# Threshold attention with a LayerNorm feed-forward block: two PSUM banks ordered by hand, and the order of work around a Strassen chain

## The chip, the cores and the metric

The kernel runs on one core of a Trainium2 chip. The metric is the device time of one execution in microseconds. A core has five engines with a queue of instructions each: TensorE (PE in the profile; its weight loads are PEld), VectorE (DVE), ScalarE (ACT), GpSimd (POOL) and SyncE (SP), which issues most DMAs. Engines wait for each other by semaphores.

## The reference

Attention over 8 batches, 8 heads, 576 tokens and 64 features per head, in which only the scores within `tau` of the row's largest are kept. Then, per token over all 512 features, a normalisation, a hidden layer of 2048 with a ReLU, and a sum with the input:

```python
scores = scale * np.matmul(q, k.transpose(0, 1, 3, 2))
thresh = np.max(scores, axis=-1, keepdims=True) - tau
scores = np.where(scores >= thresh, scores, -1000000000.0)
attn = np.exp(scores - np.max(scores, axis=-1, keepdims=True))
attn = attn / (np.sum(attn, axis=-1, keepdims=True) + 1e-09)
x = heads_side_by_side(np.matmul(attn, v))          # (8, 576, 512)
xn = (x - mean(x)) / np.sqrt(var(x) + 1e-06) * g_ln
out = x + np.maximum(xn @ w_ch1, 0.0) @ w_ch2
```

All arithmetic on the chip is in float32. The weights come as float64 bits and are turned into float32 in the kernel.

## The kernel before

**Attention in slots.** The attention of one batch is nine slots, 72 in all (n = 0 to 71). A slot handles 256 query rows of two heads, or, in the fifth slot of a batch, the last 64 rows of every head. In a slot, TensorE makes the scores (L414) into two score tiles `sc`, VectorE reduces their negated maxima (`neg`, L433), GpSimd makes the thresholds (`thr`, L437), ScalarE makes four exponentials (L445) into a room `e`, VectorE masks and sums them (L454), GpSimd divides them (L470), and VectorE transposes them in blocks of 32 (L539, two instructions). Then a DMA writes them to DRAM (`scr`, L547), and others read them back in another order (`em` at L561, `er` at L566). The values matmuls of the slot (L605, L615) run one slot later. Slots 0 to 5 do the transposition on TensorE (`tp`, `tr`) instead.

There are two rooms for `e`. Slots 0 to 6 use them in turns; from slot 7 on all use room 0, and room 1 is taken over: first as two pieces in which raw weights are fetched (`conversion.take`), later, from group 1's first part on, for one of the sums of weights. The exponentials of a slot can only be written to a room when the `scr` DMA of the slot that used it has landed.

**Feed-forward groups.** Half a batch, 288 tokens, is a group, 16 in all (g = 0 to 15). Even groups are ready after the batch's fifth slot, odd ones after its ninth. The mean comes from a matmul with a constant matrix (`mean_of`), and VectorE subtracts it (`centre`, L680). `first_part` makes the hidden layer in tiles of 128 hidden features (`p1`, 16 matmul instructions each, then a ReLU on ScalarE, L917). Groups from 2 on do eight such tiles (t = 0 to 7), and the other half of the hidden layer in a `chain`: a Strassen product, two rounds of seven segments of 16 matmul instructions, in which a pair of banks is copied out by ScalarE after each segment (L857 to L883) while later segments go on adding into the same bank. Four of the segments in each round need a difference or a sum of inputs (`turns`, L821), and three per round need an add and a maximum afterwards (`rectify`, L842 and L843, on GpSimd). The variance is a square on ScalarE (L923), three adds on GpSimd (L925), a matmul (`var`) and three activations (L937 to L939). The second product of groups from 1 on is a Strassen product too (`second_quarters`, seven segments `seg` of 64 matmul instructions each, copied out at L1012).

**The order.** It is written out by hand, and engines follow it. Each slot has four quarters; in each, `second_part` issues as many steps of the feed-forward generator as its share (`ROOM`) allows, in between the slot's own work:

```python
rest = exponentials(n)                      # neg, thr
for _ in range(0 if chained[0] else 2):     # two exponentials at once
    next(rest)
second_part(n, 0)
while not chained[0] and next(held, None):  # the other two
    pass
second_part(n, 1)
diags = weights(es, thr, blocks_go)         # masks
second_part(n, 2)
scr = turn_blocks(b, s, room)               # L539 and the scr DMA
run(n, 3)                                   # values of the slot before
second_part(n, 3)
```

While `chained[0]` is set, an exponential is issued only after each finished tile or segment. VectorE's and GpSimd's closing work of a group's second product (adds, `finish` at L1047 and L1039, transposes of the output at L723) is kept in a list, `drops`, and issued in portions; `drip(everything=True)`, which `chain` calls first, issues all that is left. Of the odd groups from 3 to 13, tile 0 is begun in quarter 0 of a batch's third slot, and seven drops (two `finish`, one add, four output transposes) wait at that time.

**The banks.** Of the banks of PSUM, six hold the two score tiles with the values' outputs behind them. Two are left for everything else; they are a pool with two buffers under one tag (`ff`), and the framework chooses which of the two a new tile gets.

Of the kernel before, what the change touches and what calls it, by code (L numbers as in the profile page):

```python
# [18 lines left out]
def kernel(  # L19
# [39 lines left out]
    J = 4  # L59
# [15 lines left out]
    ps_sc = ctx.enter_context(tc.tile_pool(name="ps_sc", bufs=1, space=bass.MemoryType.PSUM))  # L75
    ps_ff = ctx.enter_context(tc.tile_pool(name="ps_ff", bufs=2, space=bass.MemoryType.PSUM))

# [110 lines left out]
    class Weights:  # L188
# [13 lines left out]
        def __init__(self):  # L202
# [29 lines left out]
            for t, n, before in (  # L232
# [7 lines left out]
                for p in range(n):  # L240
# [3 lines left out]
                    )  # L244

        def take(self, t):
            for p in range(2):
                self.free.append((2 * self.n1, -1, t[:, p * 2 * WC : (p + 1) * 2 * WC], 99))

# [174 lines left out]
    def exponentials(n):  # L424


        neg = small.tile([128, 4], F32, tag="neg", name="neg")
        thr = small.tile([128, 4], F32, tag="thr", name="thr")
        room = e_room[(n + 1) % 2 if n <= FIRST else 0]
        es = by_columns(room) if by_blocks(n) else by_rows(room)  # L430
        for h in range(2):
            i = slice(2 * h, 2 * h + 2)
            nc.vector.tensor_reduce(  # L433
                out=neg[:, i], in_=pairs[h],
                axis=AXL.X, op=ALU.max, negate=True,
            )
            nc.gpsimd.tensor_scalar(  # L437
                out=thr[:, i], in0=neg[:, i], scalar1=-1.0, scalar2=low_sb,
                op0=ALU.mult, op1=ALU.add,
            )  # L440
            if h == 0 and not chained[0]:
                run(n, "copy")
        for i in range(4):
            yield room, es, thr
            nc.scalar.activation(  # L445
                es[:, i], as_in(es, blocks[i]), func=AF.Exp, bias=neg[:, i : i + 1]
            )
# [36 lines left out]
    def turn_weights(s, es, diags):  # L484
# [3 lines left out]
        for i in range(4):  # L488
            if i:
                yield  # L490
            tp = ps_ff.tile([128, J, 128], F32, tag="ff", name="tp")
            for c in range(J):
                product(
                    tp[:, c], lhsT=es[:, i, c * 128 : (c + 1) * 128], rhs=diags[i],
                    start=True, stop=True,
                )
            if s == HP:
                nc.scalar.copy(
                    em[:, :, :, 32 * i : 32 * i + 32].rearrange("p a c x -> p c a x"),
                    tp.rearrange("p c (a x) -> p c a x", a=4),  # L500
                )
            else:
                h, j = divmod(i, 2)
                nc.scalar.copy(
                    em[:, 2 * j : 2 * j + 2, :, 64 * h : 64 * h + 64].rearrange("p a c x -> p c a x"),
                    tp.rearrange("p c (a x) -> p c a x", a=2),
                )
        tr = ps_ff.tile([128, 2, 128], F32, tag="ff", name="tr")
        for i in range(4):
# [69 lines left out]
    def values_of(b, s, turned_weights):  # L579
# [4 lines left out]
        if at_once:  # L584
            both = ps_ff.tile([128, 2, 128], F32, tag="ff", name="pv")
            pv = [both[:, j] for j in range(2)]
# [79 lines left out]
    def mean_of(g):  # L666
        if banks_taken[0]:
            waiting_mean.append(g)
            return
        means[g] = ps_ff.tile([128, TOK], F32, tag="ff", name="mean")  # L670
        product(means[g], lhsT=avg_sb, rhs=sums.pop(g), start=True, stop=True)

    def centre(g):
# [5 lines left out]
        for c in range(NK):  # L679
            nc.vector.tensor_tensor(  # L680
                out=xc[:, c], in0=groups[g][:, c], in1=mean, op=ALU.subtract
            )


# [118 lines left out]
    def chain(g, xc):  # L803
# [24 lines left out]

        def segment(bank, weights, rhs, ds, first):
            for i, d in enumerate(ds):  # L830
                for c in range(2):
                    at, end = (i, c), (len(ds) - 1, 1)
                    product(
                        bank[:, i], lhsT=weights(c, d), rhs=rhs[:, c],
                        start=first and at == (0, 0), stop=at == end,
# [4 lines left out]

        def rectify(eng, t, other):
            eng.tensor_tensor(out=t, in0=t, in1=other, op=ALU.add)  # L842
            eng.tensor_scalar(  # L843
                out=t, in0=t, scalar1=0.0, scalar2=1.0, op0=ALU.max, op1=ALU.mult
            )

        for n, at in enumerate(range(0, len(CHAIN), 2)):
            ds = CHAIN[at : at + 2]
            banks = [ps_ff.tile([128, 2, HT], F32, tag="ff", name="ch") for _ in range(2)]
            one, two = banks if n % 2 == 0 else banks[::-1]  # L850
            up, down = (hidden[:, ds[0] + o : ds[0] + o + 2] for o in (0, ND // 2))
            m1, u2, m7 = (None,) * 3
            part_tile = lambda name: ffn.tile([128, HM, HT], F32, tag="part", bufs=4, name=name)
            chained[0] = True
            yield from segment(one, a11, b11, ds, True)
            m1 = part_tile("m1")
            nc.scalar.copy(m1, one)  # L857
            yield 2, 0.5
            yield from segment(two, a12, b21, ds, True)
            nc.scalar.copy(up[:, :, early], two)  # L860
            rectify(nc.gpsimd, up[:, :, early], m1)
            yield 2, 0.5
            yield from segment(one, s2, t2, ds, False)
            u2 = part_tile("u2")
            nc.scalar.copy(u2, one)
            yield 2, 0.5
            yield from segment(two, s3, t3, ds, True)
            m7 = part_tile("m7")
            nc.scalar.copy(m7, two)
            yield 2, 0.5  # L870
            yield from segment(one, s1, t1, ds, False)
            if n == 1:
                while len(rooted) <= g:
                    run_all(aside)
            nc.scalar.copy(down[:, :, late], one)
            rectify(nc.gpsimd, down[:, :, late], m7)
            yield 2, 0.5
            yield from segment(two, a22, t4, ds, False)
            nc.scalar.copy(down[:, :, early], two)
            rectify(nc.gpsimd, down[:, :, early], u2)  # L880
            yield 2, 0.5
            yield from segment(one, s4, b22, ds, False)
            nc.scalar.activation(up[:, :, late], one, func=AF.Relu)  # L883
            if at + 2 >= len(CHAIN):
                chained[0] = False
            yield 2, 0.5

    def first_part(g):
# [13 lines left out]
        for t, d in enumerate(tiles):  # L902
            while conversion.carried < 4 * (d // 4 + 1):
                yield 0, 0
            while d == ND - 2 and len(rooted) <= g and not plain:
                run_all(aside)
            if chains and t == last - 1:
                next(chains)
            p1 = ps_ff.tile([128, TOK], F32, tag="ff", name="p1")
            for c in range(NK):  # L910
# [8 lines left out]
            yield 2, 1  # L919
            if sq is None and t and (part > 1 or t == (4 if chains else ND // 2 - 1)):  # L920
                squared = t
# [4 lines left out]
            elif sq is not None and rb is None and (  # L926
                t >= squared + (7 if plain else 3) and part > (0 if plain else 1)
                or t == (last if chains else ND - NK - 1)
            ):
                var = ps_ff.tile([128, TOK], F32, tag="ff", name="var")  # L930
                product(var, lhsT=avg_sb, rhs=sq[:, 0], start=True, stop=True)
# [18 lines left out]
    def second_plain(g, rb):  # L950
        for m in range(NK):
            p2 = ps_ff.tile([128, TOK], F32, tag="ff", name="p2")
            for d in range(ND):
# [13 lines left out]
    def second_quarters(g, rb):  # L967
# [31 lines left out]
        def segment(weights, rhs, out=None):  # L999
            bank = ps_ff.tile([128, HM, HT], F32, tag="ff", name="seg")  # L1000
            for d in range(HD):
                for m in range(HM):
                    at, end = (d, m), (HD - 1, HM - 1)
                    product(
                        bank[:, m], lhsT=weights[:, m, d], rhs=rhs[:, d],
                        start=at == (0, 0), stop=at == end,
# [3 lines left out]
            if out is None:  # L1010
                out = ffn.tile([128, HM, HT], F32, tag="part", bufs=4, name="part")
            nc.scalar.copy(out, bank)  # L1012
            if g == 1:
# [3 lines left out]
        def last_tiles(weights, rhs):  # L1017


            for m in range(HM):  # L1020
                bank = ps_ff.tile([128, HT], F32, tag="ff", name="end")
                for d in range(HD):
                    product(
                        bank, lhsT=weights[:, m, d], rhs=rhs[:, d],
                        start=d == 0, stop=d == HD - 1,
# [4 lines left out]
                z = ffn.tile([128, HT], F32, tag="part", bufs=4, name="z")  # L1030
                dve.tensor_tensor(out=z, in0=bank, in1=rb[:, late], op=ALU.mult)
                add(dve, y12[:, m], y12[:, m], z)
# [163 lines left out]
    def constants(times):  # L1196

        warm = ps_ff.tile([128, QH], F32, tag="ff", name="warm")
        for _ in range(times):
# [19 lines left out]
    for n in range(NS):  # L1219
# [65 lines left out]
        if blocks_go:  # L1285
            conversion.fetch(0 if n == FIRST + 2 else 3, wait=0)
            conversion.prepare_to(end_at, False)
            scr = turn_blocks(b, s, room)
            if n == FIRST:
                at_quarter(n + 1, 0, conversion.take, e_room[1])  # L1290
            conversion.carry_all()
# [81 lines left out]
```

## Time and profile before

| | |
|---|---|
| median of 3 runs | 1367.58 us (1366.32 to 1371.47) |
| the profiled execution, its own time | 1367.19 us |
| its span, first to last instruction | 1365.1 us |
| mean granted clock of TensorE | 0.994 |
| TensorE busy | 1300.3 us |
| VectorE, GpSimd, ScalarE busy | 908.4, 816.0, 489.7 us |
| maxima of the scores (L433), 144 | 1351 ns each |
| exponentials (L445), 288 | 754 ns each |
| masks (L454), 288 | 810 ns each |
| block transposes (L539), 132 | 1374 ns each |
| `rectify` on GpSimd: L842, 84, and L843, 84 | 824 or 801 ns, and 1185 ns each |

A busy time is the union of an engine's instructions. The span is a few slots of start with conversion of weights, then a pattern that repeats for each batch, some 160 us, and an end without attention. A wait belongs to the instruction that stood, with the engine and line that ended it.

### The profile page before, as it was taken

The page shows a single profiled execution, that of the slowest core. Times are in us where ns is not written, and L with a number is a line of the kernel's source. Part 1 is how long each engine was busy: PE and PEld are TensorE (multiplying, and loading weights), DVE is VectorE, ACT ScalarE, POOL GpSimd, SP SyncE. Part 2 cuts the span into 40 slices and gives each one's busy share as a digit, 9 for nine tenths or more (in the row PEclk, how much of TensorE's full clock was granted, in tenths as well). Part 3 has the DMA queues.
Part 4 walks back from the last instruction along what each step waited for, and adds up shares of the span by engine and source line. Part 5 has one row for each costly group of instructions (what it writes and reads, how often), then busy time and mean ns, then how long its engine had stood idle before and what let it go on. Part 6 is the DMA issues. An engine that isn't in the chain of part 4 may idle for free. (4 is left out here: it accounts for less than half of the span.)

```text
span 1365.1 us, 43424 instructions
## 1 busy us (share of the span) xinstructions
PE 1300.3 (95%) x18648; PEld 1055.0 (77%) x18648; DVE 908.4 (67%) x1583; ACT 489.7 (36%) x1079; POOL 816.0 (60%) x1036
## 2 busy tenths in 40 slices
PE   8897899999999999999999999999999999999997
PEld 7664557879697887968788786977869687787977
DVE  7879876767765676675767577556766667566313
ACT  5864332242433323233333423323242333324130
POOL 3565556566574746657574664747466574755654
PEclk9998999999999999999999999999999999999999
DMA  8937664447644574537735476444754377443311
GB/s 167 303 109 187 161 161 148 176 132 203 179 149 145 170 215 132 183 110 191 215 115 171 135 205 188 142 152 136 206 164 161 107 191 198 149 149 138 92 19 19
DMA packets 335311, 214.11 MB, mean 157 GB/s; under 512 B 247376, under 2 KB 292688, under 8 KB 327056
## 3 DMA queue, kind: packets, MB, share of 16 engines
q1 hardware_dynamic: 329008, 210.46, 53.0%
q8 instruction: 146, 2.39, 0.7%
q10 hardware_dynamic: 5952, 0.74, 0.4%
q14 instruction: 45, 0.37, 0.1%
q0 software_dynamic: 160, 0.15, 0.1%
HBM read 124.00 MB, written 87.29 MB: 155 GB/s over the span
## 5 line engine op out<-in xcount | busy, mean ns | idle before, releaser
L433 DVE TENSOR_REDUCE neg<-sc 128x2 f32<-128x1152 f32 x144 | 188.6, 1351 | 198.0 <-PE sc L414 197.5
L112 PE MATMUL p<-xc,w 128*64 128x288 f32 x2304 | 292.5, 408 | 8.2 <-ACT part L1012 4.0
L470 POOL TENSOR_SCALAR e<-e,den 128x576 f32<-128x576 f32 x264 | 200.0, 770 | 104.3 <-DVE den L459 104.3
L112 PEld LDWEIGHTS p<-xc,w 128*64 128x64 f32 x2304 | 162.1, 137 | 126.2 <-issue 11.1
L112 PE MATMUL seg<-hidden,w 128*64 128x144 f32 x3840 | 248.2, 287 | 4.3 <-ACT part L1012 2.6
L112 PEld LDWEIGHTS seg<-hidden,w 128*64 128x64 f32 x3840 | 234.9, 137 | 11.4 <-issue 6.9
L454 DVE SCALAR_TENSOR_TENSOR e<-sc,thr,e 128x576 f32<-128x576 f32 x288 | 222.5, 810 | 23.8 <-POOL thr L437 10.1
L445 ACT ACTIVATE e<-sc,neg 128x576 f32<-128x576 f32 x288 | 201.8, 754 | 38.8 <-DMA scr<-e 34.2
L539 DVE STREAM_TRANSPOSE e<-e 128x1152 f32<-128x1152 f32 x132 | 180.4, 1374 | 41.8 <-POOL e L470 40.8
L437 POOL TENSOR_SCALAR thr<-neg,low_sb 128x2 f32<-128x2 f32 x144 | 40.1, 279 | 208.8 <-DVE neg L433 206.3
L414 PE MATMUL sc<-kT,qT 64*64 64x384 f32 (+3 forms) x2048 | 140.3, 403 | 3.2 <-DVE e L454 3.2
L605 PE MATMUL sc<-em,v_in 128*64 128x128 f32 (+1 forms) x2368 | 132.0, 264 | 6.1 <-DVE e L454 5.6
L605 PEld LDWEIGHTS sc<-em,v_in 128*64 128x64 f32 x2368 | 122.2, 137 | 12.7 <-DVE e L454 8.5
L112 PE MATMUL seg<-hidden,stage 128*64 128x144 f32 x1920 | 124.6, 287 | 0.0
L112 PEld LDWEIGHTS seg<-hidden,stage 128*64 128x64 f32 x1920 | 117.3, 137 | 5.2 <-issue 5.2
L628 ACT COPY x<-sc 128x128 f32<-128x128 f32 x120 | 32.0, 269 | 235.4 <-PE sc L414 171.1
L917 ACT ACTIVATE hidden<-p 128x288 f32<-128x288 f32 x144 | 59.7, 415 | 157.1 <-PE p L112 155.5
L414 PEld LDWEIGHTS sc<-kT,qT 64*64 64x64 f32 x2048 | 76.3, 133 | 44.8 <-issue 21.3
L843 POOL TENSOR_SCALAR hidden<-hidden 128x288 f32<-128x288 f32 x84 | 99.6, 1185 | 7.7
L1012 ACT COPY part<-seg 128x288 f32<-128x288 f32 x74 | 30.0, 406 | 189.2 <-PE seg L112 189.1
L997 POOL TENSOR_TENSOR hidden<-hidden 128x576 f32<-128x576 f32 x60 | 87.3, 1476 | 6.8 <-DVE hidden L997 6.8
L997 DVE TENSOR_TENSOR hidden<-hidden 128x576 f32<-128x576 f32 x60 | 57.8, 999 | 38.6 <-POOL hidden L997 20.9
(155 smaller groups left out, 1713.5 us busy)
## 6 DMA issues: line engine op xcount, KB each, us to landing
scr<-e SPq DMA_DIRECT2D x63, 1152.0 KB, 5.0
em<-scr SPq DMA_DIRECT2D x63, 1024.0 KB, 5.7
out_dram<-ot SPq DMA_DIRECT2D x248, 36.0 KB, 3.8
q_in<-in_q_dram SPq DMA_DIRECT2D x120, 72.0 KB, 2.6
er<-scr SPq DMA_DIRECT2D x132, 64.0 KB, 5.1
k_in<-in_k_dram SPq DMA_DIRECT2D x116, 72.0 KB, 2.9
v_in<-in_v_dram SPq DMA_DIRECT2D x28, 256.0 KB, 5.4
w<-in_moe_w_ch_dram SPq DMA_DIRECT2D x11, 512.0 KB, 6.8
```

The source lines that it names most:

```text
L112: nc.tensor.matmul(out[r], lhsT=lhsT[:, r], rhs=rhs, **flags)
L414: nc.tensor.matmul(sc[h][64 * i : 64 * i + 64, at : at + n], lhsT=ql[r] if s == HP else qT[half][r, j * 128 + 64 * i : j * 128 + 64 * i + 64],
L433: nc.vector.tensor_reduce(out=neg[:, i], in_=pairs[h], axis=AXL.X, op=ALU.max, negate=True,)
L437: nc.gpsimd.tensor_scalar(out=thr[:, i], in0=neg[:, i], scalar1=-1.0, scalar2=low_sb, op0=ALU.mult, op1=ALU.add,)
L445: nc.scalar.activation(es[:, i], as_in(es, blocks[i]), func=AF.Exp, bias=neg[:, i : i + 1])
L454: nc.vector.scalar_tensor_tensor(out=es[:, i], in0=as_in(es, blocks[i]), scalar=thr[:, i : i + 1], in1=es[:, i], op0=ALU.is_ge, op1=ALU.mu ...
L470: nc.gpsimd.tensor_scalar(out=es[:, i], in0=es[:, i], scalar1=den[:, i : i + 1], scalar2=1.0, op0=ALU.mult, op1=ALU.mult,)
L539: nc.vector.transpose(two, two)
L605: nc.tensor.matmul(dst[64 * h : 64 * h + 64], lhsT=vt[:, h, c, :], rhs=pick(em[:, 2 * j : 2 * j + 2, c], h), start=c == 0 and first, stop= ...
L843: eng.tensor_scalar(out=t, in0=t, scalar1=0.0, scalar2=1.0, op0=ALU.max, op1=ALU.mult)
L917: nc.scalar.activation(hidden[:, d], p1, func=AF.Relu)
L997: eng.tensor_tensor(out=out[at], in0=in0[at], in1=in1[at], op=op)
```

## The change

It has five parts.

1. The two free banks become two fixed tiles. `bank()` hands them out in turns, and `next_bank(t)` puts the bank of `t` next. It is called by `centre` for the mean's bank (not in group 0) and after each round of the chain.
2. `next(chains)`, whose first step empties the drops and issues the turns, comes two tiles before the last (t = 5) and not one (t = 6), and `chained[0]` is set there and not at the chain's first segment.
3. The square may come one tile sooner (t = 3), and `var` at the latest at t = 6, not 7.
4. `rectify` runs on VectorE. It is put into a list, `due`, and issued after the copy of a later segment, though not in quarter 0 of a slot.
5. Slots 7 and 8 of the first batch use the two rooms for `e` in turns too, and room 1 is no longer given to the conversion.

```diff
-    ps_ff = ctx.enter_context(tc.tile_pool(name="ps_ff", bufs=2, space=bass.MemoryType.PSUM))
+    ps_ff = ctx.enter_context(tc.tile_pool(name="ps_ff", bufs=1, space=bass.MemoryType.PSUM))
+    ff = [ps_ff.tile([128, 512], F32, name=f"ff{i}") for i in range(2)]
+    ff_order = [0, 1]
+    def bank(*shape):
+        b = ff_order.pop(0)
+        ff_order.append(b)
+        if len(shape) == 1:
+            return ff[b][:, : shape[0]]
+        return ff[b][:, : shape[0] * shape[1]].rearrange("p (a c) -> p a c", a=shape[0])
+    def next_bank(t):
+        b = [x.tensor.name for x in ff].index(t.tensor.name)
+        ff_order.remove(b)
+        ff_order.insert(0, b)
...
-        def take(self, t):
-            for p in range(2):
-                self.free.append((2 * self.n1, -1, t[:, p * 2 * WC : (p + 1) * 2 * WC], 99))
...
-        room = e_room[(n + 1) % 2 if n <= FIRST else 0]
+        room = e_room[(n + 1) % 2 if n < SLOTS else 0]
...
                 out=xc[:, c], in0=groups[g][:, c], in1=mean, op=ALU.subtract
             )
+        if g:
+            next_bank(mean)
...
-        def rectify(eng, t, other):
-            eng.tensor_tensor(out=t, in0=t, in1=other, op=ALU.add)
-            eng.tensor_scalar(
+        due = []
+        def rectify(t, other):
+            nc.vector.tensor_tensor(out=t, in0=t, in1=other, op=ALU.add)
+            nc.vector.tensor_scalar(
                 out=t, in0=t, scalar1=0.0, scalar2=1.0, op0=ALU.max, op1=ALU.mult
             )
+        def out_of(bank_, to=None, relu=False, then=None):
+            if to is None:
+                to = ffn.tile([128, HM, HT], F32, tag="part", bufs=4, name="part")
+            if relu:
+                nc.scalar.activation(to, bank_, func=AF.Relu)
+            else:
+                nc.scalar.copy(to, bank_)
+            if part:
+                run_all(due)
+            if then is not None:
+                due.append(lambda: rectify(to, then))
+            return to
...
-            banks = [ps_ff.tile([128, 2, HT], F32, tag="ff", name="ch") for _ in range(2)]
-            one, two = banks if n % 2 == 0 else banks[::-1]
+            one, two = bank(2, HT), bank(2, HT)
...
-            nc.scalar.copy(up[:, :, early], two)
-            rectify(nc.gpsimd, up[:, :, early], m1)
+            out_of(two, up[:, :, early], then=m1)
...
-            nc.scalar.activation(up[:, :, late], one, func=AF.Relu)
+            out_of(one, up[:, :, late], relu=True)
+            next_bank(two)
             if at + 2 >= len(CHAIN):
+                run_all(due)
                 chained[0] = False
...
-            if chains and t == last - 1:
+            if chains and t == last - 2:
                 next(chains)
+                chained[0] = True
-            p1 = ps_ff.tile([128, TOK], F32, tag="ff", name="p1")
+            p1 = bank(TOK)
...
-            if sq is None and t and (part > 1 or t == (4 if chains else ND // 2 - 1)):
+            if sq is None and t and (part > 1 or t == (3 if chains else ND // 2 - 1)):
...
-                or t == (last if chains else ND - NK - 1)
+                or t == (last - 1 if chains else ND - NK - 1)
             ):
-                var = ps_ff.tile([128, TOK], F32, tag="ff", name="var")
+                var = bank(TOK)
...
-            if n == FIRST:
-                at_quarter(n + 1, 0, conversion.take, e_room[1])
```

All other tiles of the pool (`tp`, `tr`, `pv`, `mean`, `p2`, `seg`, `end`, `warm`) become calls of `bank` in the same way.

## The prediction

> **What bounds the kernel now.** The page's first part comes first, then TensorE's waits from the chain-of-waits view (engine, line, who was waited for: microseconds in total, times, longest).
>
> ```profile
> PE 1300.3 (95%) x18648; PEld 1055.0 (77%) x18648; DVE 908.4 (67%) x1583; ACT 489.7 (36%) x1079; POOL 816.0 (60%) x1036
> ...
> PE ch L112 <- ACT hidden L917: 11.2, 6, 2.0
> PE p L112 <- ACT hidden L917: 6.5, 2, 5.9
> PE p L112 <- ACT part L1012: 4.0, 7, 0.6
> PE ch L112 <- ACT hidden L937: 2.7, 6, 0.5
> ```
>
> TensorE is busy for 1300.3 of 1365.1 us, so any gain must come from the 65 us in which it stands. 11.2 + 2.7 = 13.9 us of that are six equal stalls at the head of a chain, one in each odd group from 3 to 13. 5.9 us is one stall in slot 8, and 4.0 us are seven starts of a group. The timeline shows the anatomy of an odd group's stall (group 5, slots 29 and 30; start, length, engine).
>
> ```profile
> 514.42 1.38 DVE L539 STREAM_TRANSPOSE e<-e 128x1152 f32<-128x1152 f32 x1
> 516.07 1.38 DVE L539 STREAM_TRANSPOSE e<-e 128x1152 f32<-128x1152 f32 x1 [0.28 <-POOL e L470]
> 517.48 0.36 SPq L547 DMA_DIRECT2D scr<-e  x1
> 521.54 0.84 DVE L723 STREAM_TRANSPOSE ot<-y 128x288 f32<-128x288 f32 x2 [3.54 <-POOL y L1039]
> 523.17 0.84 DVE L723 STREAM_TRANSPOSE ot<-y 128x288 f32<-128x288 f32 x2 [0.79 <-POOL y L1039]
> 524.54 0.94 DVE L821 TENSOR_TENSOR turns<-turns,xc 128x288 f32<-128x288 f32 x1
> 525.40 2.61 DVE L433 TENSOR_REDUCE neg<-sc 128x2 f32<-128x1152 f32 x2
> 526.95 1.38 ACT L445 ACTIVATE e<-sc,neg 128x576 f32<-128x576 f32 x2
> 528.21 0.42 ACT L917 ACTIVATE hidden<-p 128x288 f32<-128x288 f32 x1
> 528.68 1.20 PE L112 MATMUL ch<-xc,w 128*64 128x144 f32 x16 [1.83 <-ACT hidden L917]
> 530.33 1.20 PE L112 MATMUL ch<-xc,w 128*64 128x144 f32 x16 [0.46 <-ACT hidden L937]
> ```
>
> The last tile's ReLU (L917) stands behind two exponentials, and the var's Identity (L937) behind two more. TensorE loses 1.83 + 0.46 = 2.29 us. The upper rows matter more below: the block transposes of the weights (L539) end at 517.45, their DMA goes out at once, and only then do the output transposes (L723) wait for GpSimd.
>
> Two more stretches: slot 8, and the granted clock by windows (PEclk).
>
> ```profile
> 125.93 1.37 ACT L445 ACTIVATE e<-sc,neg 128x576 f32<-128x576 f32 x2 [6.34 <-DMA scr<-e]
> 127.75 3.63 PE L112 MATMUL p<-hidden,w 128*64 128x288 f32 x14 [5.88 <-ACT hidden L917]
> ...
> 126.90:133.70 6.80, 5.95 (x26) 3.38 (x28) 6.62 (x16) 4.50 (x9) 2.78 (x3) 0.50 1.01 266
> 850.60:853.90 3.30, 2.98 (x26) 2.94 (x28) 3.08 (x9) 1.84 (x5) 0.27 (x1) 0.50 0.00 0
> ```
>
> **Exponentials one by one, var sooner.** In slot 30 the order on ScalarE becomes var's three activations, ReLU, one exponential, copy of segment one, exponential, copy, and so on. That removes both waits: 6 x 2.29 = 13.7 us, if the exponentials can start on time.
>
> They can't, I think, because next(chains) moves too, from tile 6 to tile 5. The first call of chain() empties all drops, then issues the four turns. Where does tile 5 begin? Slot 29 issues 92 matmuls of p at 506.40 before its values matmuls at 517.61, which open quarter 3. A tile is 16, so 92 are 5.75 tiles: tile 5 begins in quarter 2, tile 6 in quarter 3. turn_blocks (L539 and the scr DMA) comes between these quarters. So seven drops that came after L539 now come ahead of it: two finishes on GpSimd, one add and four output transposes on VectorE, and then two turns on each.
>
> GpSimd can't be earlier with them. Its finishes run 518.62 to 523.14, directly behind the normalisations (L470) and square sums (L925), which keep their order. So VectorE, in program order, still does output transposes at 521.54 and 523.17 and turns until 525.48; then only L539, 525.5 to 528.2 (2 x 1.38), eleven microseconds late. Behind L539 on VectorE stand the neg reductions (528.2 instead of 525.4). Behind the scr DMA on SP stand em and er. The scr DMA landed 5.0 us after its issue in one slot and 6.0 here (517.48 to 523.50): now at 533.2 to 534.2. Since e has one room from slot 9 on, the first exponential of slot 30 waits for that landing.
>
> Now the one-by-one order turns against the kernel: the copy of segment one stands behind that exponential. TensorE does var and tile 7 (524.2 to 526.9) and two segments (1.02 each, to 528.95). Segment three adds into bank one and needs the copy: 533.7 + 0.74 (exponential) + 0.27 (x copy) + 0.40 + 0.06 = 535.2. That is a stall of 6.2, plus 0.4 us where copies and exponentials (1.16 a segment against 1.02) then hold TensorE back: 6.6. Net of the 2.29 removed it is +4.3 a group, 6 x 4.3 = **+26**. Bounds: 5.5 to 7.3 us a stall, +19 to +30. em lands 5.9 us after its issue (523.58 to 529.46), so at 539.6; the values matmuls that need it come at 541, and no second stall follows. Even groups begin tile 5 in quarter 1, as they did tile 6; nothing passes L539 there. Group 15 has no drops left.
>
> **The clock.** After the 5.88 us stall the clock stood at half for 6.8 us, after one of the six 2.29 us stalls for 3.4. At half, 68 matmuls of p took 11.4 us, against 0.127 each (40 in 5.07): 2.8 lost. The short one lost 1.5. For each new stall I take 2.0 (bounds 0 and 2.8): 6 x 2.0 - 1.5 = **+10.5**. The Trainium skill, TensorE: Matmul & The Clock Gate, part 1 (the HAM clock gate), has the clock halved only after an idle window of about 3.4 us. The row at 850 differs, since 2.29 us were enough there. By the rule the dip at 850 would not have come from that stall; a stall over 6 us may still hold a whole idle window.
>
> **Two rooms in slot 8.** The 6.34 us wait of the exponentials goes, and with it 5.88 us of TensorE and 2.8 at half clock: at most 8.7. What is late next: the values matmuls at 138.96 need em, which landed at 132.7, so 6.2 is left. Then VectorE: it begins slot 9's reductions 1.2 us after its last piece of slot 8. That slot's L539 waited 1.4 us for GpSimd (136.99); ahead of it stands conversion work that doesn't move, so 1.4 is all that it gains. Slot 9's weights, for which TensorE waited 2.50 at 158.96, hang on VectorE. I take 1.2 + 1.4 = **-2.6**, bounds 0 and -8.7. The two raw chunks that lose e_room[1] (fetched at 104.89) now wait for pieces that GpSimd frees near 110; they are first needed at 152.6.
>
> **Banks by hand.** An even group's first tile took the bank of the last segment, free when ScalarE's copy ended. It now gets the mean's.
>
> ```profile
> 423.45 1.53 DVE L680 TENSOR_TENSOR xc<-x,mean 128x288 f32<-128x288 f32 x4
> ...
> 424.11 0.40 ACT L1012 COPY part<-seg 128x288 f32<-128x288 f32 x1 [2.54 <-PE seg L112]
> ...
> 424.56 5.07 PE L112 MATMUL p<-xc,w 128*64 128x288 f32 x40 [0.57 <-ACT part L1012]
> ```
>
> That bank is free when all four subtractions have read it, at 424.98, not 424.51: +0.47 in six groups, up to +1.1 in group 2 (the same four rows there end at 264.9, TensorE started at 263.95): **+4**, bounds 0 and +4.5. Odd groups already used the mean's bank.
>
> **Sums on VectorE.** 84 adds (480 ns, from L1039) and 84 maxima (between 288 and 512 ns, from a 128x512 tensor_scalar at 512) are 65 to 83 us more on VectorE; GpSimd loses 46.1 + 22.4 + 99.6 = 168. VectorE stays under 73%. On the path: in slot 26 two pairs (1.8 us) now precede the masks. These began at 462.56, behind q_in's scaling at 460.96, which stood behind two sums on GpSimd; without them it can run at 458.6, after the x copy and its add. The 2.3 us won pay for the pairs. Three pairs (2.6 us) precede L539, delay scr by 2.2 and the exponentials of slot 27, which already waited 1.0 for it; the copy behind them then costs 0.3 or so. Together **0**, bounds -3 and +5.
>
> **Sum.** 26 + 10.5 - 2.6 + 4 + 0 = +37.9. From the profiled execution's 1367.19 (span 1365.1) that makes 1405.1; its time is 0.4 under the median. I say **1405**.
>
> **Rivals.** (a) Not slower: L539 is done before the drops after all, or GpSimd, without the sums, finishes sooner. The point is slot 30's first exponential at about 527.4: if scr lands by then, all six stalls go. -13.7 - 1.5 - 2.6 + 4 = -13.8, so 1353. For it: L539 had its inputs at 516.04. Against: the matmul count puts tile 5 in quarter 2, and this stretch holds none of the sums. 0.13. (b) The stall comes, but the clock holds: -12 and 1393. For it: five of six stalls of 2.29 us left the clock alone. 0.22. (c) Stalls of 3.8 us with full slot 8 gains: 9 - 1.5 - 6.2 + 4 = +5, so 1372. 0.05. (d) The change isn't what it says: GpSimd's sums do go, but that was no wait of TensorE's; the price is inside the 0 above.
>
> **How the numbers follow.** The main case, stall and clock, has 0.60. Its bounds are 19 - 1.5 - 8.7 + 0 - 3 = +6 and 30 + 15.3 + 0 + 4.5 + 5 = +55, which don't all fall together: 1385 to 1420. With (b) and half of (c) the range is 1374 to 1422. About 0.5% is what a measurement of this kernel can tell from no change. Faster 0.13, within 0.05, slower 0.82.
>
> **What would show it.** Right: in odd groups L539 stands behind L723 and L821; ch waits some 6 us for ACT's part copies, ACT e for DMA scr grows from 34 us to over 60; half clock follows these stalls; slot 8's 5.88 is gone. Wrong: L539 at its old place and no long ch wait, which is rival (a); or a time over 1422, which would mean that em's landing or the masks on VectorE also stop TensorE.

## The result and the profile after

The changed kernel took 1412.77 us (median of 4 runs, 1411.98 to 1413.98) against 1366.95 (4 runs, 1366.06 to 1371.47). The ratio is 1.0329, with a 95% interval of 1.0304 to 1.0354. The profiled execution took 1412.13, with a span of 1410.4 and a mean granted clock of 0.982 instead of 0.994. In the code after, line numbers are shifted: the block transposes L539 are now L552, exponentials L445 are L458, output transposes L723 are L738, turns L821 are L836, and all chain copies go through one line, L870.

The page of the changed kernel, busy times and the group of exponentials:

```profile
PE 1312.5 (93%) x18648; PEld 1067.5 (76%) x18648; DVE 978.9 (69%) x1751; ACT 489.7 (35%) x1079; POOL 656.4 (47%) x868
...
L458 ACT ACTIVATE e<-sc,neg 128x576 f32<-128x576 f32 x288 | 202.4, 754 | 79.0 <-DMA scr<-e 73.2
```

The same group on the page of the kernel before:

```profile
L445 ACT ACTIVATE e<-sc,neg 128x576 f32<-128x576 f32 x288 | 201.8, 754 | 38.8 <-DMA scr<-e 34.2
```

TensorE runs the same 18648 matmul instructions, but is busy for 12.2 us more: that is slower clock. It stands for 1410.4 - 1312.5 = 97.9 us, 33.1 more than before. 12.2 + 33.1 is the whole 45.3 us between the spans. The exponentials' wait for the scr DMA grew from 34.2 to 73.2 us.

Where TensorE stands, from the chain-of-waits view of the changed kernel (microseconds in total, times, longest):

```profile
PE ff L129 <- ACT part L870: 30.3, 6, 6.2
PE ff L129 <- ACT y L1035: 21.6, 7, 4.5
PE ff L129 <- DVE xc L693: 11.9, 10, 2.3
```

Two more lines of that view in the kernel before:

```profile
PE sc L605 <- DVE e L454: 5.6, 6, 1.1
PE p L112 <- DVE xc L680: 3.1, 2, 1.8
```

The first line is the odd groups' stall, where 13.9 us became 30.3: +16.4. The second is new, seven even groups, with no counterpart before: +21.6. The third is the start of groups on the mean's bank, where 4.0 (for ACT's copies) and 3.1 (two starts on L680) became 11.9: +4.8. Slot 8 lost its 6.5 and got 2.1 for em: -4.4. The wait of the values matmuls for the masks (L605 for L454, 5.6 us in six times before) is gone. Together that is +32.8 of the 33.1.

**The odd groups.** The timeline of group 5, slots 29 and 30 (start, length, engine):

```profile
531.60 0.84 DVE L738 STREAM_TRANSPOSE ot<-y 128x288 f32<-128x288 f32 x2 [6.74 <-POOL y L1062]
...
535.46 2.62 DVE L552 STREAM_TRANSPOSE e<-e 128x1152 f32<-128x1152 f32 x2
...
538.15 0.36 SPq L560 DMA_DIRECT2D scr<-e  x1
...
542.39 0.74 ACT L458 ACTIVATE e<-sc,neg 128x576 f32<-128x576 f32 x1 [5.25 <-DMA scr<-e]
...
543.64 4.11 PE L129 MATMUL ff<-turns,chain_sb 128*64 128x144 f32 x32 [5.00 <-ACT part L870]
```

The block transposes now stand behind the output transposes, which wait 6.74 us for GpSimd, and behind the turns, which end at 535.54. Their DMA goes out at 538.15, the first exponential starts 4.24 us later, segment one's copy comes behind it at 543.18, and TensorE behind that. The six stalls measure 4.67 to 6.24 us.

**The even groups.** The timeline of group 4, slots 26 and 27, from the last mask on:

```profile
470.21 0.44 DVE L859 TENSOR_TENSOR hidden<-hidden,part 128x288 f32<-128x288 f32 x1
...
472.29 3.05 POOL L1020 TENSOR_TENSOR hidden<-hidden 128x576 f32<-128x576 f32 x2
472.40 1.66 DVE L859 TENSOR_TENSOR hidden<-hidden,part 128x288 f32<-128x288 f32 x1
...
474.10 1.41 DVE L860 TENSOR_SCALAR hidden<-hidden 128x288 f32<-128x288 f32 x1
...
475.43 2.63 DVE L552 STREAM_TRANSPOSE e<-e 128x1152 f32<-128x1152 f32 x2
...
483.60 1.37 ACT L458 ACTIVATE e<-sc,neg 128x576 f32<-128x576 f32 x2 [4.00 <-DMA scr<-e]
...
485.40 4.83 PE L129 MATMUL ff<-hidden,stage 128*64 128x144 f32 x48 [3.69 <-ACT y L1035]
```

And the kernel before, in the same slots:

```profile
467.55 1.38 DVE L539 STREAM_TRANSPOSE e<-e 128x1152 f32<-128x1152 f32 x1 [0.27 <-POOL e L470]
...
469.22 2.12 PE L414 MATMUL sc<-kT,qT 64*64 64x384 f32 x32
...
474.03 1.38 ACT L445 ACTIVATE e<-sc,neg 128x576 f32<-128x576 f32 x2 [1.00 <-DMA scr<-e]
```

Three pairs of add and maximum stand ahead of the block transposes. The first two (to 472.48) take 1.2 and 1.1 us. The third begins while GpSimd makes a difference of two blocks of the hidden layer for the second product (L1020, two instructions), and takes 3.1: its instructions end about when GpSimd's do. The transposes end at 478.05, 2.4 us after TensorE's scores of the next slot (475.69); in the kernel before they ended at 468.93, 2.4 us ahead of them (471.34). The scr DMA is late by these 4.8 us, and the copy that TensorE needs (484.86) stands behind two exponentials that wait for it.

**The clock.** Windows of the changed kernel; PEclk is the third column from the right. The first begins in the odd stall shown above, the second at the end of an even stall of 3.23 us:

```profile
541.00:547.80 6.80, 4.16 (x36) 4.11 (x38) 3.41 (x11) 3.80 (x9) 2.19 (x3) 0.50 0.71 224
825.50:828.90 3.40, 3.37 (x55) 3.40 (x57) 3.33 (x11) 1.45 (x3) 1.70 (x3) 1.00 0.99 319
```

Half clock, of 3.4 or 6.8 us, began within or just behind each of the six odd stalls and three of the six even ones of 3 us or so and more (4.51, 3.69 and 3.00 us; not 3.23, 2.99 and 3.22; the seventh is under 1 us).

**Banks.** The timeline of group 6's start in the changed kernel:

```profile
597.84 1.53 DVE L693 TENSOR_TENSOR xc<-x,ff 128x288 f32<-128x288 f32 x4
...
599.42 2.89 PE L129 MATMUL ff<-xc,w 128*64 128x288 f32 x22 [1.05 <-DVE xc L693]
```

The last segment's copy (598.49, 0.40 us) ends at 598.89, the subtractions at 599.37, and TensorE starts behind the latter, after 1.05 us instead of 0.57.

### The profile page after: what moved, and what is told of

Its sections match the earlier page's. It is cut to its first block, busy times and chain, and to the rows that moved or that the text cites. A ratio compares the mean times of both kernels' runs of the same rounds, so it can differ in the third digit from the quotient of the medians.

```text
span 1410.4 us, 43414 instructions
## 1 busy us (share of the span) xinstructions
PE 1312.5 (93%) x18648; PEld 1067.5 (76%) x18648; DVE 978.9 (69%) x1751; ACT 489.7 (35%) x1079; POOL 656.4 (47%) x868
## 4 chain that ended last, share of the span: by engine, by line
PE 45%; DVE 17%; DMA 10%; POOL 7%; issue 5%; SPq 2%; ACT 1%; DVEq 0%; POOLq 0%; ACTq 0%
PE ff L129 33%; DMA scr<-e 6%; PE sc L427 5%; PE sc L618 5%; DVE e L467 5%; DVE e L552 3%; DVE neg L446 2%; POOL e L483 2%; SPq L146 1%; DVE hidden L860 1%; DVE hidden L859 1%; DMA em<-scr 1%; POOL y L1062 1%; DMA v_rest<-in_v_dram 1%; POOL y L1070 1%
## 5 line engine op out<-in xcount | busy, mean ns | idle before, releaser
L129 PE MATMUL ff<-xc,w 128*64 128x288 f32 (+1 forms) x3200 | 352.3, 374 | 12.5 <-DVE xc L693 11.3
L129 PEld LDWEIGHTS ff<-xc,w 128*64 128x64 f32 x3200 | 216.6, 137 | 134.6 <-DVE xc L693 14.0
L446 DVE TENSOR_REDUCE neg<-sc 128x2 f32<-128x1152 f32 x144 | 188.1, 1347 | 186.1 <-PE sc L427 185.6
L129 PE MATMUL ff<-hidden,w 128*64 128x144 f32 (+1 forms) x4096 | 282.7, 295 | 9.3 <-POOL w L330 4.6
L483 POOL TENSOR_SCALAR e<-e,den 128x576 f32<-128x576 f32 x264 | 205.6, 790 | 162.7 <-DVE den L472 162.7
L129 PEld LDWEIGHTS ff<-hidden,w 128*64 128x64 f32 x4096 | 253.3, 137 | 31.1 <-issue 10.1
L458 ACT ACTIVATE e<-sc,neg 128x576 f32<-128x576 f32 x288 | 202.4, 754 | 79.0 <-DMA scr<-e 73.2
L450 POOL TENSOR_SCALAR thr<-neg,low_sb 128x2 f32<-128x2 f32 x144 | 40.2, 280 | 342.7 <-DVE neg L446 339.4
L552 DVE STREAM_TRANSPOSE e<-e 128x1152 f32<-128x1152 f32 x132 | 177.9, 1365 | 8.7 <-POOL e L483 8.3
L129 PE MATMUL ff<-hidden,stage 128*64 128x144 f32 x1920 | 131.1, 296 | 20.6 <-ACT y L1035 20.6
L129 PEld LDWEIGHTS ff<-hidden,stage 128*64 128x64 f32 x1920 | 123.3, 142 | 27.3 <-issue 27.3
L940 ACT ACTIVATE hidden<-ff 128x288 f32<-128x288 f32 x144 | 59.6, 414 | 164.9 <-PE ff L129 164.8
L1020 POOL TENSOR_TENSOR hidden<-hidden 128x576 f32<-128x576 f32 x60 | 88.7, 1497 | 30.0 <-ACT hidden L868 12.1
L129 PE MATMUL ff<-turns,chain_sb 128*64 128x144 f32 x896 | 73.0, 319 | 30.3 <-ACT part L870 30.3
L1035 ACT COPY part<-ff 128x288 f32<-128x288 f32 x74 | 30.1, 406 | 190.6 <-PE ff L129 190.6
L129 PEld LDWEIGHTS ff<-turns,chain_sb 128*64 128x64 f32 x896 | 64.1, 155 | 37.2 <-ACT part L870 31.9
```

The source lines that it names most:

```text
L129: nc.tensor.matmul(out[r], lhsT=lhsT[:, r], rhs=rhs, **flags)
L446: nc.vector.tensor_reduce(out=neg[:, i], in_=pairs[h], axis=AXL.X, op=ALU.max, negate=True,)
L450: nc.gpsimd.tensor_scalar(out=thr[:, i], in0=neg[:, i], scalar1=-1.0, scalar2=low_sb, op0=ALU.mult, op1=ALU.add,)
L458: nc.scalar.activation(es[:, i], as_in(es, blocks[i]), func=AF.Exp, bias=neg[:, i : i + 1])
L483: nc.gpsimd.tensor_scalar(out=es[:, i], in0=es[:, i], scalar1=den[:, i : i + 1], scalar2=1.0, op0=ALU.mult, op1=ALU.mult,)
L552: nc.vector.transpose(two, two)
```

## The experiments

The theory is that two of the five parts do the harm, each by delaying the block transposes and so the scr DMA: the place of next(chains) in odd groups, and the sums on VectorE in even ones. The rivals are that one stall makes the other, or that a third part (the order one by one, the list `due`, the banks) is needed for it.

### Undoing each, and both

The first kernel puts `next(chains)` back:

```diff
-            if chains and t == last - 2:
-                next(chains)
-                chained[0] = True
+            if chains and t == last - 2:
+                chained[0] = True
+            if chains and t == last - 1:
+                next(chains)
```

> The changed kernel with the chain's first step (drops emptied, turns issued) back at tile 6; the one-by-one mode still begins at tile 5. Theory (in odd groups the output transposes and turns pass the block transposes and so delay the scr DMA): the six waits of TensorE for the copy of segment one, 30.3 us, fall to under 2 us; the half clock behind them goes too (some 12 us); L552 is again ahead of the output transposes; 1412.8 - 30 - 12 = about 1371 us. Rival (the copies merely stand behind exponentials one by one, or VectorE is late with its added sums): the six stalls stay within 1 us each and the time within 5 us of 1412.

The second puts `rectify` back on GpSimd (still issued from `due`):

```diff
-            nc.vector.tensor_tensor(out=t, in0=t, in1=other, op=ALU.add)
-            nc.vector.tensor_scalar(
+            nc.gpsimd.tensor_tensor(out=t, in0=t, in1=other, op=ALU.add)
+            nc.gpsimd.tensor_scalar(
```

> The changed kernel with the chain's adds and maxima on GpSimd again, at the places where the change issues them. Theory (in even groups three pairs ahead of the block transposes on VectorE delay scr, so the exponentials of the next slot and the copy y behind them): TensorE's waits for ACT y, 21.6 us, fall under 3 us, the odd groups' 30 us stay, the values' wait for masks comes back with up to 5 us; about 1412.8 - 19 - 4 of clock + 4 = 1393 us. Rival (the even stall comes from the banks or from the later scr of the odd groups): ACT y stays near 20 us and the time within 5 us of 1412.

The third has both edits:

> Both edits: chain's first step at tile 6, adds and maxima on GpSimd. Theory: both stalls go, 13.9 us of the old odd stalls too, and the start keeps its 6 us: 1367 - 13.9 - 1.5 of clock - 6 + 4 (first tile in the mean's bank) = about 1350 us. Rival (GpSimd needed the relief for the one-by-one order): 1360 to 1370 us, with stalls of 1 us or more in each group's chain.

The fourth is the kernel before with the two rooms alone:

```diff
-        room = e_room[(n + 1) % 2 if n <= FIRST else 0]
+        room = e_room[(n + 1) % 2 if n < SLOTS else 0]
...
-            if n == FIRST:
-                at_quarter(n + 1, 0, conversion.take, e_room[1])
```

> The kernel before with the two rooms in slots 7 and 8 alone, and no pieces of room 1 for the conversion. My step said -2.6 us; the changed kernel's trace reaches group 1's first tile 6.0 us sooner. If the rooms alone do that: 1361 us, with the 5.88 us stall of slot 8 replaced by one of about 2 us for em. If other parts of the change help there: 1363 to 1365 us.

| kernel | median us | ratio to before, 95% interval |
|---|---|---|
| late turns | 1383.44 | 1.0128 [1.0113, 1.0143] |
| sums on GpSimd | 1388.94 | 1.0168 [1.0151, 1.0186] |
| both | 1347.91 | 0.9873 [0.9856, 0.9889] |
| rooms alone | 1363.01 | 0.998 [0.9968, 0.9992] |

The chain-of-waits view of the kernel with late turns has the line below, and 1.6 us in six times for ACT's part copies, where 30.3 stood:

```profile
PE ff L129 <- ACT y L1036: 21.7, 7, 4.5
```

That of the one with sums on GpSimd has 0.4 us in one wait for ACT y, where 21.6 stood, and this line:

```profile
PE ff L129 <- ACT part L870: 30.5, 6, 6.5
```

Each edit removes nearly all of its own stall and leaves the other as it was, so the two are separate. With both edits neither is left, and the kernel is faster than before: what remains of the change is worth a gain. The second and third kernels came near their expected numbers; the first is some 12 us over, for two reasons. TensorE's idle time fell by 23.1 us and not by nearly 30, since its waits for other copies of the chain (hidden, L870) grew from 4.6 to 9.8 us, one of them 2.51 us long. And its busy time fell by 5.6 us and not by 12: five of the six even stalls are now followed by half clock, not three, and the wait of 2.51 us by another stretch. The times don't add: alone the two cost 35.5 and 41.0 us over the version without them, together 64.9. In the profiled executions somewhat over half of that difference is in the busy time (10.7 and 12.1 us alone, 16.3 together), the rest in idle time.

The rooms alone hold the whole early gain: group 1's first tile begins at 173.65 in that kernel, 173.55 in the changed one and 179.56 before. In the median they are worth 3.3 us (1.1 to 4.4 by the interval), so the start is that of the first expectation and the time that of the second; where the rest of the 6 goes is not shown.

### Each alone in the kernel before

Moving only the call, in the kernel before:

```diff
-            if chains and t == last - 1:
+            if chains and t == last - 2:
                 next(chains)
```

> The kernel before, with next(chains) alone moved from t == 6 to t == 5. First theory (the place of the call is the whole cause of the odd groups' stalls): VectorE's block transposes stand behind the output transposes and turns in groups 3, 5, ... 13, scr lands some 11 us later, and the ReLU of tile 7 stands behind two exponentials that wait for it. Six stalls of some 7 to 9 us in place of 2.29, with a half-clock stretch behind most of them: 1400 to 1415 us. Rival (the stall needs the copies between single exponentials, which this kernel lacks): the two exponentials of slot 30 wait, the ReLU is hidden by the four turns' time, and the time is at most 1370 us.

It took 1407.29 us, ratio 1.0294 [1.0278, 1.0309]. Six stalls add up to 43.4 us, 7.1 to 7.3 each. Its timeline of slots 29 and 30:

```profile
531.13 2.63 DVE L539 STREAM_TRANSPOSE e<-e 128x1152 f32<-128x1152 f32 x2
...
538.08 1.37 ACT L445 ACTIVATE e<-sc,neg 128x576 f32<-128x576 f32 x2 [2.78 <-DMA scr<-e]
...
539.81 4.06 PE L112 MATMUL ch<-xc,w 128*64 128x144 f32 x32 [7.26 <-ACT hidden L917]
```

The place of the call alone is enough for the stall, and the order one by one, which the prediction made a part of it, makes it shorter: with exponentials in pairs tile 7's ReLU waits for scr, and TensorE stands 7.26 us; one by one it has two segments to do before it stands 5.0. Each of the six comes with 6.8 us of half clock.

Moving only the sums, in the kernel before, each pair directly behind its copy:

```diff
-            rectify(nc.gpsimd, up[:, :, early], m1)
+            rectify(nc.vector, up[:, :, early], m1)
...
-            rectify(nc.gpsimd, down[:, :, late], m7)
+            rectify(nc.vector, down[:, :, late], m7)
...
-            rectify(nc.gpsimd, down[:, :, early], u2)
+            rectify(nc.vector, down[:, :, early], u2)
```

> The kernel before, with the rectify pairs on VectorE at their old places. First theory (three pairs on VectorE ahead of the block transposes of slots 27, 36, ... make the scr transfer of every even group's second slot late): waits of TensorE for ACT at the start of the second product or at its first segment, 3 to 4.5 us in each of seven even groups, half clock behind some, 1385 to 1397 us; odd groups without a new stall. Rival (VectorE has room for the pairs, and it is the bunching of the pairs behind a later copy that makes it late): within 5 us of 1366.

1375.85 us, ratio 1.0068 [1.0044, 1.0091]. Neither answer came true, and this was the miss that mattered: no stall of 3 us at the start of an even group's second product, only longer waits for chain copies (4.0 us before, 14.4 now), 9 us in the median. So VectorE alone isn't the cause, and suspicion moved to the list `due`. Two kernels settled it. One is the version with late turns, with the list left out:

```diff
-                due.append(lambda: rectify(to, then))
+                rectify(to, then)
```

> The version with late turns and sums on VectorE (1383.4 us), with every rectify pair issued directly behind its copy instead of from the list due. First theory (the list holds a pair back until it stands ahead of the block transposes of the even groups' second slot, three there instead of two): TensorE's wait for ACT y (21.7 us in seven) goes or falls under 1 us each, 1352 to 1362 us, which is the version with sums on GpSimd (1347.9) plus the 9 us that the pairs cost in the order of before. Rival (the copies between single exponentials make the stall, wherever the pairs stand): ACT y stays near 3 us each, 1375 to 1385.

The other is the kernel before with sums on VectorE and with the list:

```diff
-            rectify(nc.vector, up[:, :, early], m1)
+            due.append(lambda t=up[:, :, early], o=m1: rectify(nc.vector, t, o))
```

(and so for the other two, `run_all(due)` behind each later copy as in the change)

> The kernel before, with the rectify pairs on VectorE and issued from the list due (the version without the list took 1375.9 us). First theory (the list makes the even groups' stall): a wait for ACT of 2 us or more at the end of the first part of six or seven even groups, 1385 to 1395 us. Rival (the list alone does no harm as long as exponentials go in pairs, since no copy stands between them): 1372 to 1380.

Without the list 1356.11 us instead of 1383.44 (ratio to before 0.9914 [0.9894, 0.9934]); with it, in the order of before, 1394.67 instead of 1375.85 (1.0206 [1.019, 1.0222]). Without it TensorE's waits for ACT y fell from 21.7 us in seven to 3.4 in three, the longest 1.90, so the stall is nearly gone, though not all of it is under 1 us, as the first theory had it. With it, in the order of before, the chain-of-waits view has the stall:

```profile
PE seg L112 <- ACT y L1026: 20.2, 6, 4.1
```

The timeline of the version without the list shows what the list did (slot 26, from the last mask):

```profile
458.68 0.44 DVE L859 TENSOR_TENSOR hidden<-hidden,part 128x288 f32<-128x288 f32 x1
...
460.29 0.66 DVE L860 TENSOR_SCALAR hidden<-hidden 128x288 f32<-128x288 f32 x1
...
460.75 2.85 POOL L1021 TENSOR_TENSOR hidden<-hidden 128x576 f32<-128x576 f32 x2
...
460.87 2.62 DVE L552 STREAM_TRANSPOSE e<-e 128x1152 f32<-128x1152 f32 x2
```

Here three pairs precede the masks and two the block transposes, and these begin 2.2 us after the first of the two, just as GpSimd takes up its differences of the hidden layer. The list holds one pair back; as a third it meets those differences, and the transposes begin 5.2 us after the first pair. These 3 us are about the size of the stall.

### The rest of the change

Plain banks, from the version with both edits:

```diff
-        if g:
-            next_bank(mean)
```

> The version with late turns and sums on GpSimd (1347.9 us), without next_bank(mean) after the subtractions. First theory: the first tile of an even group gets the last segment's bank and starts 0.5 us sooner in six groups and 1.0 us sooner in group 2; some 4 us less, 1344. Rival (the start is given back at the next tile, or the turn of the two banks is out of step in odd groups): 1347 to 1350.

1344.31 us, ratio 0.9835 [0.982, 0.9849], the fastest of all versions tried; 3.6 us less than with the mean's bank. The timeline of group 6's start in it:

```profile
573.72 0.40 ACT L1034 COPY part<-ff 128x288 f32<-128x288 f32 x1 [2.54 <-PE ff L129]
...
574.17 5.07 PE L129 MATMUL ff<-xc,w 128*64 128x288 f32 x40 [0.57 <-ACT part L1034]
```

From that version on, the exponentials' order was put back:

```diff
-            if chains and t == last - 2:
-                chained[0] = True
...
             ds = CHAIN[at : at + 2]
             one, two = bank(2, HT), bank(2, HT)
+            chained[0] = True
```

> The version with late turns, sums on GpSimd and plain banks (1344.3 us), with chained[0] set at the chain's first segment again, so that the exponentials beside tiles 6 and 7 go in pairs. First theory (the order one by one is what removed the six stalls of before): some 1.8 us of wait for ACT hidden at the head of each odd chain, 1354 to 1358 us with a little clock. Rival (var's earlier place removed them): 1344 to 1347.

and then the square and var as well:

```diff
-t == (3 if chains else ND // 2 - 1)
+t == (4 if chains else ND // 2 - 1)
...
-or t == (last - 1 if chains else ND - NK - 1)
+or t == (last if chains else ND - NK - 1)
```

> The same as the version before it in this call, with the square and var at their old tiles as well. First theory: the six stalls are back in full, 2.29 us each, one of them with a half-clock stretch, 1357 to 1361 us, so that parts 2's order and 3 together are worth some 14 us. Rival: less than 3 us over the version with var sooner, or as fast as 1344 to 1347 if neither matters.

1361.04 (0.9958 [0.9942, 0.9974]) and 1359.71 (0.9953 [0.9937, 0.9969]). The order one by one is worth about 16 us; an earlier var adds nothing that can be told from zero when exponentials go in pairs. The first kernel is over its expected range of 1354 to 1358, but the rival, 1344 to 1347, is out. In it TensorE has six stalls again, 11.7 us in all, now for var's Identity (L958), which stands behind two exponentials; with var at its old tile they are for the last tile's ReLU and var together, as before.

Last, the sums on VectorE in odd groups only, in the version with both edits:

```diff
-            nc.gpsimd.tensor_tensor(out=t, in0=t, in1=other, op=ALU.add)
-            nc.gpsimd.tensor_scalar(
+            (nc.vector if g % 2 else nc.gpsimd).tensor_tensor(out=t, in0=t, in1=other, op=ALU.add)
+            (nc.vector if g % 2 else nc.gpsimd).tensor_scalar(
```

> The version with late turns and sums on GpSimd (1347.9 us), with the rectify pairs on VectorE in odd groups only. First theory (the pairs cost only where they stand ahead of block transposes whose transfer is already waited for, which is slot 27 and its like in even groups): no new wait of TensorE over 1 us, 1346 to 1350. Rival (VectorE is too slow beside GpSimd wherever the pairs stand): new waits of 3 us or more in odd groups, 1365 or more.

1357.02 us, ratio 0.9929 [0.9908, 0.995]: neither answer. No wait reaches 3 us, but it is 9 us slower than the version with both edits; TensorE's waits for chain copies (L870) went from 4.4 to 8.6 us. The rest stays open: the profiled execution of the version with both edits took 1351.52, 3.6 over its median, so the two traces are closer than the medians.

## Why the prediction was right, and where it was not

The median came 7.8 us above the forecast, and the profiled execution 7.0 above the 1405.1 of the sum. By the terms, in profiled executions: odd groups 16.4 - 26 = -9.6, clock 12.2 - 10.5 = +1.7, slot 8 -4.4 + 2.6 = -1.8, banks 4.8 - 4 = +0.8, sums on VectorE 16 - 0 = +16, together +7.1. Two large errors of opposite sign stand behind a near number: that it is so near is in part luck.

1. **Odd groups, +26.** The mechanism is shown, by the trace and by undoing it: transposes behind drops and turns, scr late, a copy behind the waiting exponential. The size was +16.4. A stall was put at 6.6 us and measured 5.05 on average; the mis-sized term is the landing of scr, taken as 5.0 to 6.0 us, and 4.24 to 4.26 in five of the six groups. Where it took 5.67 (group 7) the stall was 6.24.
2. **The clock, +10.5.** TensorE's busy time grew by 12.2 us. All six odd stalls halved the clock, as assumed, and the size per stall was right too: with sums on GpSimd, where only the odd stalls are left, TensorE is busy for 1308.3 us, against 1296.2 with both edits, which is 12.1 or 2.0 a stall. But part of the 12.2 of the changed kernel belongs to the even stalls, which weren't foreseen. Rival (b), that the clock holds, is out.
3. **Two rooms, -2.6.** The wait for em that was named as next came, 2.1 us. But group 1's first tile began at 173.55 instead of 179.56, 6.0 us sooner. The term was too small for the start, within its bounds of 0 to -8.7; in the median the edit by itself gave about 3 us, near the term.
4. **Banks, +4.** Right, and shown twice: 1.05 instead of 0.57 us in group 6, and 3.6 us won by leaving it out.
5. **Sums on VectorE, 0, bounds -3 and +5.** This step failed. It counted the pairs rightly, two ahead of the masks and three ahead of the transposes, and priced three pairs at 2.6 us. They took 5.2, so that scr came 4.8 us later against TensorE's work, not 2.2, and 21.6 us of stall with its share of half clock came out. The add's price was the mean of 74 adds (L1039), most of which ran beside no instruction of GpSimd. Yet the profile of before had rows with such company, shown below: VectorE's own differences of the hidden layer (L997) take 0.75 us in the median, but one that begins just behind GpSimd's takes 1.95. In return the values matmuls stopped waiting for the masks (5.6 us), also unforeseen. With both in one, 21.6 - 5.6, the term was +16 before the clock.

The rows of before that step 5 could have used, one of eight such places (timelines of GpSimd and of VectorE):

```profile
394.10 2.79 POOL L997 TENSOR_TENSOR hidden<-hidden 128x576 f32<-128x576 f32 x2
395.55 1.95 DVE L997 TENSOR_TENSOR hidden<-hidden 128x576 f32<-128x576 f32 x1
```

The Trainium skill, SBUF — State Buffer, section Who interferes with whom, states the rule for step 5: a VectorE instruction with two inputs from SBUF, or a tensor_scalar in a two-port mode, contends with a GpSimd instruction that reads SBUF, and the later one waits until the earlier is done. The trace agrees: the add that began 0.11 us behind the first of GpSimd's two instructions took 1.66 us, and add and maximum together lasted 3.1 us, as those two did (3.05). By that rule, and with the 2.79 us that two such instructions took on GpSimd before, the third pair would have been estimated at about 3 us. No run here moved GpSimd's differences, so that the shared port is behind it is argued, not shown; that the third pair's lateness makes the stall is shown by the versions without the list.

Rival (a), no slowdown, had the sign wrong, but its 1353 was a fair estimate of the other parts: with both edits undone the kernel takes 1347.91.

## What to carry to other kernels

When work is moved to an engine that has idle time, look at what runs on its neighbour at that very moment: the same pair of instructions cost 0.8 us alone and 3.1 beside GpSimd's two-input differences, and a transfer behind it came too late. When a step is moved past another, list everything that its first call issues on every engine, for here four output transposes that waited for GpSimd went ahead of the one transfer on which the next slot hangs. A change in five parts should be run with each harmful part undone: the order one by one, the two rooms and the earlier var are good or neutral here, and the version with late turns, GpSimd's sums and plain banks beats the kernel before (ratio 0.9835, 0.982 to 0.9849).

## What the runs showed of the hardware

VectorE's instructions beside GpSimd, over all 84 of each in the changed kernel (shortest, median, longest in ns):

```profile
L859 DVE TENSOR_TENSOR hidden<-hidden,part x84: 414/452/1664, 285.6 to 1375.5; 128x288 f32<-128x288 f32 x84
```

```profile
L860 DVE TENSOR_SCALAR hidden<-hidden x84: 309/310/1422, 286.0 to 1376.0; 128x288 f32<-128x288 f32 x84
```

The maximum, with one tensor input, is slowed too. Of the 84, the 60 that overlap no instruction of GpSimd take 309 to 311 ns, as do 3 beside its thresholds (L450); 13 that overlap its divisions (L483) take 655 to 750, and 8 that overlap its differences (L1020) alone take 1405 to 1422.

The clock is not a function of the stall's length alone. In the kernel with `due` in the order of before, a stall of 1.84 us at 372.70 was followed by half clock, one of 2.05 at 538.82 was not:

```profile
373.90:377.30 3.40, 2.94 (x26) 2.91 (x27) 3.26 (x11) 1.98 (x6) 2.81 (x4) 0.50 0.02 5
539.00:542.40 3.40, 2.91 (x44) 2.37 (x44) 3.30 (x12) 3.00 (x7) 1.79 (x3) 1.00 0.05 10
```

In the changed kernel stalls of 3.69 us and more were always followed by it, those near 3 us in one of four. The clock records of the traces show what decides. Within each execution all half-clock stretches after the first 20 us begin on one grid of 3.41 us, and what counts is how long TensorE stands within one cell of that grid. The cells of the two stalls above, and those of a stall of 3.00 us (followed by half clock) and of 3.23 us (not) in the changed kernel; the second number is TensorE's busy time:

```profile
370.48:373.89 3.41, 1.57 (x20) 0.93 (x16) 3.01 (x5) 3.08 (x7) 1.26 (x3) 1.00 0.59 140
537.73:541.14 3.41, 1.87 (x27) 1.60 (x29) 2.97 (x9) 3.35 (x8) 1.25 (x3) 1.00 0.41 69
```

```profile
650.24:653.65 3.41, 1.31 (x22) 1.04 (x18) 2.79 (x6) 0.91 (x2) 0.99 (x2) 1.00 0.83 226
820.89:824.30 3.41, 1.42 (x24) 1.15 (x20) 2.96 (x7) 0.57 (x1) 1.16 (x3) 1.00 0.94 269
```

TensorE stands for 1.84 and 2.10 us in the cells that are followed by half clock, for 1.54 and 1.99 in the other two: a stall that an edge of the grid divides does less. Over the fourteen traces (cells at full clock, without the first 20 us and the last 15), all 57 cells with more than 2.02 us of standing were followed by half clock, and none with less than 1.83; between the two 11 of 26 were. The six stalls of 2.29 us in the kernel before put 1.66 to 1.89 us into one cell, and the one behind which the prediction saw half clock has the most. The Trainium skill, TensorE: Matmul & The Clock Gate, part 1, names an idle window of about 3.4 us; the rows here stand against reading that as the least stall, or as a window that must be idle from end to end.
